# Attention with hashed masks and an FFN on one core: the FFN's chunks start four steps earlier, on a step of their own

## The chip, the cores and the metric

The kernel runs on one core of one Trainium2 chip. Its time is the device time in microseconds (us) of one execution. Three executions of the kernel before took 989.38, 991.98 and 992.04 us; their median is 991.98 us.

## What is computed

For each of 4 batches and 8 heads, attention over 768 positions with 64 numbers per head. A query sees only the keys whose 6 hash bits (signs of a projection) equal its own. The result of the 8 heads, 512 numbers per position, goes through an FFN with 2048 inner units:

```python
q_bits = (np.einsum('bhsd,dk->bhsk', q, proj) > 0).astype(np.int64)
k_bits = (np.einsum('bhsd,dk->bhsk', k, proj) > 0).astype(np.int64)
...
mask = q_bucket[:, :, :, None] == k_bucket[:, :, None, :]
scores = scale * np.matmul(q, k.transpose(0, 1, 3, 2))
scores = np.where(mask, scores, -1000000000.0)
...
attn = attn / (np.sum(attn, axis=-1, keepdims=True) + 1e-09)
return np.matmul(attn, v).astype(np.float32)
...
h = x @ w_in
relu6 = np.clip(h + 3.0, 0.0, 6.0)
g = h * relu6 / 6.0
return (g @ w_out).astype(np.float32)
```

## The kernel before, in words

**Precision.** TensorE multiplies in a reduced float format, so most operands are kept as a high part (a copy, ScalarE mostly) and a low part (the original minus the high part, VectorE or POOL), and products are sums of two or three matrix products. High and low parts are ph/pl for attention weights, xh/xl for the FFN's input, gb or ga (two halves of one tile) for the gated values, kk/qq for a head's keys and queries.

**Attention.** The 32 heads make 192 steps of 128 queries each; step k belongs to head k // 6. `scores` (L376, L378) makes a step's 768 scores s in PSUM; `lowest` (L385, VectorE) copies them to p and finds the extreme; `exponential` (L397, ScalarE) makes the weights. The weights must be transposed. In plain steps TensorE does it: `transp` (L407), six instructions into two banks pt, whose high and low parts are made by L464 (ScalarE) and L468 (VectorE). In mixed steps `flip` does it: VectorE transposes blocks (L418), a DMA writes them to DRAM (fd), and `move` reads them back reordered with four DMAs into one of two homes, spare and px; there ScalarE makes the high parts, VectorE the low part of the first half (L468) and POOL that of the second half (L466). `values` (L489) or `values_whole` (L501) multiply by v for two steps at a time (acc); `output` copies the result to y and DMAs it to the DRAM tensor xs, half of it by an adding DMA that POOL issues (`add`, L510).

**A head's preparation.** The rows raw come by DMA (`get_qk`); a high copy qq (L304), DMAs that move rows between partitions, two low parts kk and qq on POOL (L318), which in mixed steps wait in a list `subs` and are issued one in each odd step; then hash products z (L330 to L332) and hash bits (L341, VectorE).

**FFN.** Its inputs are chunks of 256 positions, three per batch. Batch 0 has its FFN between steps 51 and 52. The nine other chunks come from the generator `ffn`, which the step loop advances piece by piece. `begin` loads a chunk's rows xr from xs and lists small pieces of work in `side`: the reciprocal sums rc (`invert`: L549, L550), then for each of four groups of 128 rows a spread copy of rc on POOL (L559), its transposition rt (L569) and the product xr times rt on VectorE (L572). `split` makes xh (L624) and xl (L625), the low parts in turn on VectorE and POOL. Then come 16 units: `gemm1` (12 matmuls, L635), `gate` (L657 ScalarE, L658 VectorE, L663, L664) and, one unit later, `gemm2` (6 matmuls, L673 to L678). `store` scales the result and DMAs it out.

**What sets the order.** TensorE, VectorE, ScalarE and POOL do their instructions in the order in which the code issues them; SyncE's DMA queue is ordered by a scheduler at build time. Three numbers set the stages: HK = 48, the steps of one batch; GF = 2·HK + FS = 100, from which step on the order within a step changes (`lead` before `split_p`); and GT = GF + FT = 106, the first step whose weights go through `flip` and `move`. From step GT − 1 on, `beside_ffn` runs each step together with one FFN unit; its order within a step is values, `lowest` of step k + 2, the gate's second half (stage A), `exponential` and `flip` of step k + 2, `split_p` of step k − 1, `gemm1` (stage B), hash, `gemm2` and the gate's first half (stage C), scores of step k + 3, moves, a part of `subs`, side work (stage D). The FFN begins when `there(0)` holds: all values of batch 1 done (`vdone >= 96`). In plain steps each call takes one piece of `side` per step; the first `gemm1` of chunk 0 comes in step 106. Chunks 1 to 5 start in steps 122, 138, 154, 170 and 186. What is left after step 194 (55 units) runs alone.

**A detail of buffers.** In plain steps every third half of a step's parts ("extra" in `split_p`) lies in the buffers xh and xl, which the FFN's chunks use too.

Of the kernel before, what the change touches and what calls it, by code (L numbers as in the profile page):

```python
# [18 lines left out]
P = 128  # L19
# [9 lines left out]
LA = 3  # L29
FB = 4  # L30
FS = 4
FT = 6
# [11 lines left out]
def lsh_attention_moe(  # L44
# [10 lines left out]
    nc = tc.nc  # L55
# [384 lines left out]
    def split_p(g: int, c: int, third: bool):  # L440

        nonlocal halves
        u, w = divmod(g, 2)
        if w == 0:
            extra = third and halves % 3 == 2
            halves += 1
            if extra and lent:
                both = [x[:, :S] for x in lent]
            else:
                both = [  # L450
                    sp.tile([P, NCC * TC if extra else S], F32R, name=f"{x}{u}_{c}", tag=f"x{x[1]}" if extra else x, bufs=1 if extra else 2)[:, :S]
                    for x in ("ph", "pl")
                ]
            parts[u, c] = [x.rearrange("p (x w q) -> p x w q", x=QT, w=2) for x in both]
        hi, lo = (x[:, :, w] for x in parts[u, c])
        engine = nc.vector
        if g < GT:
            pt = pts.pop((g, c))[:]
        else:
            pt = moved[g].rearrange("p (i x a) -> p x i a", i=4, x=KT)[:, c * QT : (c + 1) * QT]  # L460
            hi, lo = (x.rearrange("p x (i a) -> p x i a", i=4) for x in (hi, lo))
            if c:
                engine = nc.gpsimd
        nc.scalar.copy(hi, pt)  # L464
        if engine is nc.gpsimd:
            engine.tensor_sub(lo, pt, hi.bitcast(F32))  # L466
        else:
            lows.append(lambda: engine.tensor_sub(lo, pt, hi.bitcast(F32)))  # L468
# [44 lines left out]
    def output(un: int):  # L513
# [16 lines left out]
        else:  # L530
            nc.scalar.copy(y, acc[:])
        if u:
            c = slice(0, 4 * P) if u == 1 else slice(4 * P, S)
            to = xs[b][h * D : (h + 1) * D, c]

            with tc.issue_after(copied.ins):
                dma(out=to, in_=outs[i][r])
            if not last_head:
                adds.append((i, to, outs[i][r2]))
# [25 lines left out]
    def normalise(name: str, x, rb, tag: str | None = None):  # L565
# [6 lines left out]
        muls.append(lambda: nc.vector.tensor_mul(x, x, rt[:]))  # L572
        if not paced:
            multiply()

    muls = []

    def multiply():
# [23 lines left out]
    def scale_x(b: int, t: int, ccs: range, xr, rc=None):  # L602
# [4 lines left out]
        def invert():  # L607
            piece()
            rbs["rc"] = rc if rc is not None else inverse(name, b, slice(t * TC, (t + 1) * TC), ccs)

# [90 lines left out]
    xr0, x0 = {}, {}  # L701
    side = []

# [191 lines left out]
    def ffn():  # L895
# [5 lines left out]
        def there(c: int) -> bool:  # L901

            return vdone >= (chunks[c][0] + 1) * HK

        def begin(c: int):
# [5 lines left out]
            if b < B - 1:  # L911
                side.extend([lambda: None] * (0 if paced else 2) + todo)
                return
# [18 lines left out]
        def split(c: int, cc: int):  # L932
            split_x(xhl[c][cc], xr[c][:, cc], (nc.vector, nc.gpsimd)[cc % 2])

# [70 lines left out]
    def lead(j: int):  # L1005

        i, t = divmod(j, KT)
        n = i + 1
        alone = j < GF + LA
        if t == 0 and n < NJ:  # L1010
# [55 lines left out]
    with tc.manual_schedule(engines={ET.PE, ET.DVE, ET.Activation, ET.Pool}):  # L1066
# [15 lines left out]
        def beside_ffn(k: int):  # L1082

            nonlocal paced, stage
            if k < GT:
# [3 lines left out]
            for _ in range(2):  # L1091
# [8 lines left out]
                if k < GT:  # L1100
                    break
            if k + 2 < NS and k >= GT:
                lowest(k + 2)
# [37 lines left out]

            if subs and k % 2:
                subs.pop(0)()
# [4 lines left out]
        for k in range(NS + LT + 2):  # L1148
# [23 lines left out]
            for _ in range(1 if k != HK else 2):  # L1172
                if vnext < k - k % 2:
                    whole = value_half()
            if k >= GF - 2:
                next(fill, None)
# [7 lines left out]
            for c in range(2):  # L1184
                split_p(k, c, third)
            split_lows()
            if (k < GF or hashed) and k + LA < end:
                if hashed:
# [85 lines left out]
```

## Time and profile before

| | us |
|---|---|
| median of three executions | 991.98 |
| the profiled execution | 993.35 |
| its span, first to last instruction | 991.6 |
| TensorE (PE) busy in the span | 957.5 |
| VectorE (DVE) busy | 716.1 |
| ScalarE (ACT) busy | 626.4 |
| POOL busy | 491.2 |
| mean granted TensorE clock | 0.997 |

Rows of the timeline give an instruction's start, its duration, engine, line of the kernel, operation, tiles written and read, shapes and count; in brackets the idle time of the engine just before and what ended it. Matmuls overlap in the pipe, so a row's duration is longer than the distance to the next start; what a matmul costs is that distance. Rows of the windows give, for a stretch, its length, each engine's busy time and number of instructions, the granted clock, the DMA engines' mean busy share and GB/s.

### The profile page before, as it was taken

Reading aid. Unit: us, or ns where it says so; the run is one execution under the profiler, and the core shown is the slowest. Engines: PE = TensorE matmul, PEld = TensorE weight load, DVE = VectorE, ACT = ScalarE, POOL = GpSimd, SP = SyncE. Lnnn points to the kernel's source line nnn. Section 1 sums busy time; section 2 is a strip of 40 time slices with the busy share of each in tenths; the row PEclk is TensorE's granted clock in tenths of the full one; section 3 lists DMA queues with packets and bytes.
Section 4 is the critical chain, followed back from the end, with each engine's and each line's share of the span. In section 5 each row is a group of like instructions: output and inputs, shape, how many; then the busy total and the mean of one; then the engine's idle time right before and its main releaser. Section 6 shows DMA issues by size and latency. Waiting matters only on the chain.

```text
span 991.6 us, 19371 instructions
## 1 busy us (share of the span) xinstructions
PE 957.5 (97%) x6330; PEld 877.2 (88%) x6330; DVE 716.1 (72%) x1444; ACT 626.4 (63%) x1419; POOL 491.2 (50%) x514
## 2 busy tenths in 40 slices
PE   8999999999999999799999999999999999999997
PEld 7999888999989998699889898888989989899996
DVE  7999988888479998777767877867867863343332
ACT  6888875565488887566656766666666663333332
POOL 6777745666456676365655654645645540000100
PEclk9999999999999999999999999999999999999999
DMA  4566689000035554587888787778788670101000
GB/s 117 137 163 171 141 248 376 9 1 1 27 119 119 120 121 116 139 237 234 235 249 247 221 246 231 226 223 236 240 230 247 202 213 14 43 1 43 1 22 22
DMA packets 109980, 148.51 MB, mean 150 GB/s; under 512 B 13380, under 2 KB 79300, under 8 KB 109880
## 3 DMA queue, kind: packets, MB, share of 16 engines
q1 hardware_dynamic: 105320, 141.64, 47.0%
q0 software_dynamic: 4560, 5.64, 4.7%
q8 instruction: 50, 0.82, 0.4%
q14 instruction: 50, 0.41, 0.1%
HBM read 75.76 MB, written 52.04 MB: 129 GB/s over the span
## 4 chain that ended last, share of the span: by engine, by line
PE 71%; DVE 9%; DMA 7%; POOL 4%; issue 3%; SPq 3%; ACT 2%; DVEq 0%; ACTq 0%; POOLq 0%
PE h L635 23%; PE acc L489 6%; PE po L678 6%; PE po L673 6%; PE po L674 6%; PE pt L407 5%; PE s L376 4%; PE s L378 4%; PE acc L501 4%; DMA px<-fd 3%; SPq L78 3%; DVE p L385 3%; DVE pl L468 3%; POOL pl L466 2%; DMA spare<-fd 2%
## 5 line engine op out<-in xcount | busy, mean ns | idle before, releaser
L397 ACT ACTIVATE p<-p,m 128x768 f32<-128x768 f32 x192 | 180.2, 939 | 94.8 <-DVE p L385 87.8
L385 DVE TENSOR_SCALAR_CACHE_REDUCE p<-s 128x768 f32<-128x768 f32 x192 | 182.9, 953 | 44.3 <-PE s L378 25.7
L658 DVE SCALAR_TENSOR_TENSOR h<-g,h 128x256 f32<-128x256 f32 x192 | 82.0, 427 | 108.2 <-ACT g L657 106.6
L657 ACT ACTIVATE g<-h,three 128x256 f32<-128x256 f32 x192 | 90.8, 473 | 100.0 <-PE h L635 98.2
L635 PE MATMUL h<-xh,w 128*128 128x256 f32 x1024 | 146.4, 282 | 2.7 <-ACT xh L624 2.7
L635 PEld LDWEIGHTS h<-xh,w 128*128 128x128 f32 x1024 | 135.5, 189 | 6.2 <-ACT xh L624 2.9
L418 DVE STREAM_TRANSPOSE p<-p 128x768 f32<-128x768 f32 x86 | 84.1, 978 | 56.9 <-ACT p L397 56.9
L466 POOL TENSOR_TENSOR pl<-spare,ph 128x384 fp32r<-128x384 f32 x43 | 59.1, 1375 | 114.1 <-ACT ph L464 80.1
L468 DVE TENSOR_TENSOR pl<-pt,ph 128x384 fp32r<-128x384 f32 x204 | 104.0, 549 | 3.7 <-ACT ph L464 3.2
L376 PE MATMUL s<-kk,qq 76*128 76x384 f32 x384 | 101.6, 346 | 4.1 <-DVE qq L341 2.3
L378 PE MATMUL s<-kk,qq 128*128 128x384 f32 x384 | 100.5, 343 | 0.0
L464 ACT CAST ph<-pt 128x384 fp32r<-128x384 f32 x204 | 89.5, 472 | 16.6 <-PE pt L407 13.6
L663 ACT CAST gb<-h 128x256 fp32r<-128x256 f32 x139 | 51.6, 372 | 75.6 <-DVE h L658 45.6
L673 PE MATMUL po<-w,gb 128*128 128x512 f32 x246 | 96.9, 394 | 0.2 <-ACT gb L663 0.2
L674 PE MATMUL po<-w,gb 128*128 128x512 f32 x246 | 96.9, 394 | 0.0
L407 PE MATMUL pt<-ident,p 128*128 128x128 f32 x636 | 89.5, 274 | 5.1 <-DVE pl L468 4.1
L216 POOL TENSOR_TENSOR w<-wr,w 128x128 fp32r<-128x128 f32 x128 | 71.8, 591 | 45.3 <-ACT w L210 42.5
L466 POOL TENSOR_TENSOR pl<-px,ph 128x384 fp32r<-128x384 f32 x43 | 58.4, 1357 | 60.0 <-ACT ph L464 40.1
L407 PEld LDWEIGHTS pt<-ident,p 128*128 128x128 f32 x636 | 74.6, 141 | 13.3 <-PE pt L407 3.8
L635 PE MATMUL h<-xl,w 128*128 128x256 f32 x512 | 83.4, 283 | 2.5 <-POOL xl L625 2.2
L376 PEld LDWEIGHTS s<-kk,qq 76*128 76x128 f32 x384 | 65.6, 190 | 16.4 <-DVE qq L341 6.8
L678 PE MATMUL po<-w,gb 128*128 128x512 f32 x246 | 77.4, 395 | 1.6 <-DVE gb L664 1.6
(154 smaller groups left out, 2150.1 us busy)
## 6 DMA issues: line engine op xcount, KB each, us to landing
fd<-p SPq DMA_DIRECT2D x86, 384.0 KB
spare<-fd SPq DMA_DIRECT2D x172, 96.0 KB
px<-fd SPq DMA_DIRECT2D x172, 96.0 KB
kk<-qq SPq DMA_DIRECT2D x62, 192.0 KB
wr<-in_w_in SPq DMA_DIRECT2D x16, 512.0 KB
wr<-in_w_out SPq DMA_DIRECT2D x16, 512.0 KB
raw<-in_qkT SPq DMA_DIRECT2D x20, 384.0 KB
vr<-in_v SPq DMA_DIRECT2D x32, 192.0 KB
```

The source lines that it names most:

```text
L376: nc.tensor.matmul(s[:, c, :HW], lhsT=q1[:KM, us], rhs=half(k1[:KM], c), start=True, stop=False)
L378: nc.tensor.matmul(s[:, c, :HW], lhsT=q2[:, us], rhs=half(k2, c), start=False, stop=True)
L385: nc.vector.tensor_scalar(out=pr_[:], in0=s[:, :, :HW], scalar1=CAP, scalar2=None, op0=ALU.min, op1=ALU.min, accum_out=m[:],)
L397: nc.scalar.activation(pr_[:], pr_[:], AF.Exp, bias=m[:], scale=-1.0, accum_out=sms[b][:, t, h : h + 1])
L407: nc.tensor.transpose(pt[:, x], probs[g][0][:, c, x * P : (x + 1) * P], ident[:])
L466: engine.tensor_sub(lo, pt, hi.bitcast(F32))
L468: lows.append(lambda: engine.tensor_sub(lo, pt, hi.bitcast(F32)))
L635: nc.tensor.matmul(hp, lhsT=wi[:, wp, wc], rhs=x[cc][xp], start=(k == 0 and cc == 0), stop=(k == 2 and cc == NCC - 1),)
L657: nc.scalar.activation(r[:], hp, AF.Relu, bias=three[:], scale=1.0)
L673: nc.tensor.matmul(po[u], lhsT=gh[:, us], rhs=wo[:, 0], start=(fc == 0), stop=False)
L674: nc.tensor.matmul(po[u], lhsT=gh[:, us], rhs=wo[:, 1], start=False, stop=False)
L678: nc.tensor.matmul(po[u], lhsT=gl[:, us], rhs=wo[:, 0], start=False, stop=(fc == NFC - 1))
```

## The change

Several edits go together. FS goes from 4 to 0, so that GF is 96 and GT 102. `there` asks only for the values that a chunk needs (its 256 positions) and that no adding DMA of the batch is outstanding; so that the last head of a batch can be read early, its first 256 positions are written by a DMA of their own. The pieces of a plain-step chunk come without two empty ones ahead (they are behind now), and its `place` and `split` are done at the beginning of step GT, behind that step's values, and not when the generator comes to it. In the steps before GT the multiplications by rt and the reciprocals wait until the step's low parts are issued (`held`, `multiply`). All four xl of a chunk are VectorE's. POOL's part from `subs` is left out in the last step of a chunk and done in the first step of the next. The third half that lies in xh and xl is another one of three.

```diff
-FS = 4
+FS = 0
...
-            extra = third and halves % 3 == 2
+            extra = third and halves % 3 == 1
...
-        if u:
-            c = slice(0, 4 * P) if u == 1 else slice(4 * P, S)
+        if u or last_head:
+            c = slice(2 * u * P, 2 * (u + 1) * P) if last_head and b else slice(0, 4 * P) if u == 1 else slice(4 * P, S)
...
-                dma(out=to, in_=outs[i][r])
+                dma(out=to, in_=y[r] if last_head else outs[i][r])
...
-        if not paced:
+        if not paced and not held:
             multiply()
...
-            rbs["rc"] = rc if rc is not None else inverse(name, b, slice(t * TC, (t + 1) * TC), ccs)
+            def now():
+                rbs["rc"] = rc if rc is not None else inverse(name, b, slice(t * TC, (t + 1) * TC), ccs)
+
+            if held:
+                muls.append(now)
+            else:
+                now()
...
-            return vdone >= (chunks[c][0] + 1) * HK
+            b, t = chunks[c]
+            return vdone >= (b + 1) * HK - KT + 2 * (t + 1) and not any(b * H <= a[0] < (b + 1) * H for a in adds)
...
-                side.extend([lambda: None] * (0 if paced else 2) + todo)
+                side.extend(todo + [lambda: None] * (0 if paced else 2))
+                if not paced:
+                    opening.append(lambda: (place(c), [split(c, cc) for cc in range(NCC)]))
...
-            split_x(xhl[c][cc], xr[c][:, cc], (nc.vector, nc.gpsimd)[cc % 2])
+            split_x(xhl[c][cc], xr[c][:, cc], nc.vector)
...
-        alone = j < GF + LA
+        alone = j <= GF + LA
...
+            if k == GT:
+                opening.pop()()
             if k + 2 < NS and k >= GT:
                 lowest(k + 2)
             go("A")
...
-            if subs and k % 2:
+            place_in_chunk = (k - GT) % NFC
+            if subs and (k % 2 and (k < GT or place_in_chunk != NFC - 1) or k > GT and place_in_chunk == 0):
                 subs.pop(0)()
...
-            if k >= GF - 2:
+            held = k >= GF - 2
+            if held:
                 next(fill, None)
...
             split_lows()
+            multiply()
+            held = False
```

With it chunk 0 begins its loads in step 94 and its units in step 102; chunks 1 to 5 start in steps 118, 134, 150, 166 and 182; four more steps have flipped weights, and 51 units are left for the end. In steps 96 to 99 `lead`, with the hash of head 17 in step 96, now stands ahead of `split_p`.

The order in which instructions stand shows three places. First VectorE where the FFN starts, in the kernel before: p106 and p107 are weights of the first flipped steps, pl52 the last low parts of plain steps, xl1_0 the chunk's low parts, h1_0_0 and gb1_0_0 its first gate.

```order
L468 TENSOR_TENSOR pl52_1_5641<-pt105_1_5649,ph52_1_5640 128x3x128
L418 STREAM_TRANSPOSE p106_5618<-p106_5618 128x768
L385 TENSOR_SCALAR p107_5670,m107_5669<-s107_5632 128x768
L418 STREAM_TRANSPOSE p107_5670<-p107_5670 128x768
L385 TENSOR_SCALAR p108_5708,m108_5707<-s108_5682 128x768
L572 TENSOR_TENSOR xr1_0_5400<-xr1_0_5400,rt1_0_3_5676 128x256
L418 STREAM_TRANSPOSE p108_5708<-p108_5708 128x768
L625 TENSOR_TENSOR xl1_0_5716<-xr1_0_5400,xh1_0_5715 128x256 x2
L658 SCALAR_TENSOR_TENSOR h1_0_0_5725<-g1_0_0_5741,h1_0_0_5725 128x256
L385 TENSOR_SCALAR p109_5755,m109_5754<-s109_5744 128x768
L664 TENSOR_TENSOR gb1_0_0_5757<-h1_0_0_5725,gb1_0_0_5757 128x256
```

The same place in the changed kernel, four steps earlier:

```order
L468 TENSOR_TENSOR pl50_1_5504<-pt101_1_5512,ph50_1_5503 128x3x128
L418 STREAM_TRANSPOSE p102_5486<-p102_5486 128x768
L385 TENSOR_SCALAR p103_5533,m103_5532<-s103_5495 128x768
L418 STREAM_TRANSPOSE p103_5533<-p103_5533 128x768
L632 TENSOR_TENSOR xl1_0_5563<-xr1_0_5271,xh1_0_5562 128x256 x4
L385 TENSOR_SCALAR p104_5573,m104_5572<-s104_5539 128x768
L418 STREAM_TRANSPOSE p104_5573<-p104_5573 128x768
L665 SCALAR_TENSOR_TENSOR h1_0_0_5579<-g1_0_0_5596,h1_0_0_5579 128x256
L385 TENSOR_SCALAR p105_5612,m105_5611<-s105_5601 128x768
L671 TENSOR_TENSOR gb1_0_0_5614<-h1_0_0_5579,gb1_0_0_5614 128x256
```

All four low parts of the chunk have moved ahead of one `lowest` and one `flip`, and the multiplication by rt is gone from this place.

Second POOL where chunk 3 starts (batch 2, positions 0 to 255), before: pl76_1 is the second half's low part of a step, kk_27 and qq_27 the low parts of a head, xl2_0 the chunk's.

```order
L466 TENSOR_TENSOR pl76_1_8616<-spare_5399,ph76_1_8615 128x3x128
L318 TENSOR_TENSOR kk_27_8642<-raw27_8437,qq_27_8643 64x768
L625 TENSOR_TENSOR xl2_0_8657<-xr2_0_8259,xh2_0_8656 128x256 x2
L510 DMA xs3_128<-y24_2_8561 64x256
L466 TENSOR_TENSOR pl76_1_8616<-px_5688,ph76_1_8615 128x3x128
L466 TENSOR_TENSOR pl77_1_8747<-spare_5399,ph77_1_8746 128x3x128
L318 TENSOR_TENSOR qq_27_8643<-raw27_8437,qq_27_8643 64x768
```

And in the changed kernel at the start of the same chunk:

```order
L318 TENSOR_TENSOR kk_26_8377<-raw26_8173,qq_26_8378 64x768
L559 COPY spare_5270<-rc2_0_8131 128x256
L466 TENSOR_TENSOR pl73_1_8351<-px_5544,ph73_1_8350 128x3x128
L466 TENSOR_TENSOR pl74_1_8475<-spare_5270,ph74_1_8474 128x3x128
L466 TENSOR_TENSOR pl74_1_8475<-px_5544,ph74_1_8474 128x3x128
L318 TENSOR_TENSOR qq_26_8378<-raw26_8173,qq_26_8378 64x768
```

POOL has no xl any more, and the head's part that falls into the chunk's last step stands one L466 later.

Third SyncE's DMA queue where a chunk's store, a head's rows and the next chunk's loads meet; before, at the start of chunk 2 (step 138): out is the store, raw25 the rows of a head, xr2_0 the next chunk's loads, px and spare the moves.

```order
L78 DMA raw25_7708<-in_qkT 64x768 x2
L78 DMA fd140_7673<-p140_7666 128x768
L78 DMA xs2_127<-y22_0_7566 64x512
L78 DMA px_5688<-fd139_7612 32x4x192 x2
L78 DMA out_0<-ob1_1_7704 128x512 x2
L78 DMA px_5688<-fd139_7612 32x4x192 x2
L78 DMA xr2_0_8259<-xs2_127 128x256
```

In the changed kernel at the start of chunk 3 (step 150), which has the same place within its head:

```order
L78 DMA out_0<-ob1_2_8560 128x512 x2
L78 DMA px_5544<-fd151_8469 32x4x192 x2
L78 DMA raw27_8564<-in_qkT 64x768
L78 DMA px_5544<-fd151_8469 32x4x192 x2
L78 DMA fd153_8598<-p153_8591 128x768
L78 DMA raw27_8564<-in_qkT 64x768
L78 DMA spare_5270<-fd152_8529 32x4x192
```

The head's rows, which need the buffer that the moved part of `subs` frees, have gone from ahead of the store to behind it, between the moves.

More of the change, by code (lines that the diff above doesn't have):

```diff
@@ L701, in lsh_attention_moe @@
     xr0, x0 = {}, {}
-    side = []
+    side, opening = [], []
     def beside():
@@ L1082, in beside_ffn @@
         def beside_ffn(k: int):
-            nonlocal paced, stage
+            nonlocal paced, stage, held
+            held = False
             if k < GT:
@@ L1186, in lsh_attention_moe @@
             split_lows()
+            multiply()
+            held = False
             if (k < GF or hashed) and k + LA < end:
```

## The prediction

> **What bounds the kernel now.** I read the page first, then the windows, then PE's timeline where a window shows PE idle. The page:
>
> ```profile
> span 991.6 us, 19371 instructions
> PE 957.5 (97%) x6330; PEld 877.2 (88%) x6330; DVE 716.1 (72%) x1444; ACT 626.4 (63%) x1419; POOL 491.2 (50%) x514
> PE   8999999999999999799999999999999999999997
> ```
>
> PE is the bound nearly everywhere: 34.1 us of the span are left beside its 957.5. An edit gains only by removing PE work or PE waits. Of 40 slices one in the middle shows a 7. The windows around it, one of the mixed stage, and one of the end where the FFN runs alone:
>
> ```profile
> 375.00:400.00 25.00, 22.85 (x163) 21.08 (x162) 22.43 (x45) 18.44 (x42) 14.62 (x13) 1.00 0.49 126
> 400.00:425.00 25.00, 18.88 (x118) 16.98 (x118) 18.09 (x37) 13.28 (x32) 10.77 (x11) 0.93 0.55 156
> 500.00:525.00 25.00, 23.59 (x151) 21.14 (x150) 17.25 (x32) 15.07 (x37) 11.34 (x10) 1.00 0.88 248
> 850.00:875.00 25.00, 25.00 (x163) 22.63 (x162) 7.68 (x18) 8.71 (x20) 0.00 (x0) 1.00 0.12 43
> ```
>
> The start of the FFN (375 to 425) holds 2.15 + 6.12 = 8.3 us of idle PE, a quarter of all. A bad window of the mixed stage holds 1.4, the end none. So there are three places where this change can gain: the start, the chunk starts inside the mixed stage, and PE work itself. The third window also warns: its DMA engines are 0.88 busy.
>
> **1. Transpositions that leave PE.** Four steps go over to flipped weights. A plain step's six transpositions, and what starts behind them:
>
> ```profile
> 397.66 0.82 PE L407 MATMUL pt<-ident,p 128*128 128x128 f32 x6
> 398.24 0.61 PE L489 MATMUL acc<-ph,vv 128*128 128x256 f32 x3
> ```
>
> From start to start 0.58 us; four steps give −2.3 us. The FFN units and scores of these steps only change places: PE does them either way. But a mixed step can wait where a unit at the end cannot: the first unit starts at 415.60 in step 106 and the one of step 154 at 639.11 (rows below), 48 steps of 4.66, so four mixed steps are some 19 us; and the windows of the mixed stage lose between 0 and 1.4 per 25. I take the middle, +0.5 (bounds 0 and +1.1).
>
> **2. The start of the FFN.** PE's waits, with the step before the first unit and the first scores behind it:
>
> ```profile
> 394.82 0.52 PE L407 MATMUL pt<-ident,p 128*128 128x128 f32 x3 [1.00 <-DVE pl L468]
> 401.09 0.85 PE L407 MATMUL pt<-ident,p 128*128 128x128 f32 x6 [0.97 <-DVE pl L468]
> 403.20 0.41 PE L569 MATMUL rt<-ident,spare 128*128 128x128 f32 x2 [0.55 <-ACT y L531]
> 410.36 0.44 PE L569 MATMUL rt<-ident,spare 128*128 128x128 f32 x2 [1.48 <-POOL spare L559]
> 412.06 0.87 PE L501 MATMUL acc<-pl,vv 128*128 128x256 f32 x6
> 415.60 2.36 PE L635 MATMUL h<-xh,w 128*128 128x256 f32 x8 [2.67 <-ACT xh L624]
> 418.61 0.84 PE L376 MATMUL s<-kk,qq 76*128 76x384 f32 x2
> ```
>
> The engines that it waited for there, and the granted clock just behind the longest wait:
>
> ```profile
> 393.00 0.98 DVE L549 TENSOR_SCALAR rc<-sms 128x16 f32<-128x16 f32 x1
> 397.94 1.09 DVE L341 TENSOR_SCALAR qq<-z,thr,val 44x768 fp32r<-44x768 f32 x1
> 410.22 0.92 DVE L385 TENSOR_SCALAR_CACHE_REDUCE p<-s 128x768 f32<-128x768 f32 x1
> 413.21 0.92 DVE L385 TENSOR_SCALAR_CACHE_REDUCE p<-s 128x768 f32<-128x768 f32 x1
> 417.50:418.60 1.10, 1.10 (x7) 1.10 (x6) 0.37 (x1) 0.00 (x0) 0.09 (x1) 0.50 1.07 410
> ```
>
> The waits of rt go: all four spread copies now stand on POOL ahead of head 18's preparation, and rt comes at a step's end, behind an output done earlier: −(1.48 + 0.55) = −2.0. The wait of 0.97 had a multiplication by rt ahead of pl; now it stands behind. VectorE is nearly full there (22.43 of 25), so I take half: −0.5. The 1.00 behind rc stays: rc still stands ahead of the next step's pl. New is a wait in step 96, where `lead`, and with it head 17's hash bits of 1.09, now stand ahead of that step's pl; PE's next transpositions need the banks which pl reads. Bounds 0 and +1.1; +0.7, nearer the full row, as the bits also wait for their hash.
>
> The first `gemm1` costs 2.67 of wait and, from 415.60 to 418.61, 3.01 in place of 1.40 (rows below), 4.3 in all. In that chain VectorE goes through one more `lowest`, `exponential` and `flip` round ahead of xh than the changed order does; a round is 413.21 − 410.22 = 3.0. But PE arrives 1.5 earlier, as rt doesn't wait: 2.67 − 3.0 + 1.5 leaves 1.2. Four xh follow one after the other, so the unit itself still runs slower by some 0.9: 2.1 in place of 4.3, −2.2. The round that moved behind is owed by the first gates; PE works on `gemm1` and hash meanwhile, and I take a third of it, +1.0. Sum of the start: −2.0 − 0.5 + 0.7 − 2.2 + 1.0 = −3.0. Bounds: all 8.3 gone, or +1 where new waits outweigh.
>
> The last row shows half the clock granted (0.50) behind that wait; with the wait at 1.2 I count on the full clock, and that is in the 2.1. If the half clock came back, the unit would cost its whole 3.01 − 1.40 = 1.6 over 1.40 and not 0.9, and the start would be −2.3 in place of −3.0. The Trainium skill (TensorE: Matmul & The Clock Gate, Part 1) halves the clock only after an idle window of about 3.4 us. The trace agrees on the half and not on the length: 2.67 of idle were enough. By the page's figure neither 2.67 nor 1.2 should halve it; the row decides, and by it the shorter wait is what matters.
>
> **3. Chunk starts in the mixed stage.** A unit inside a chunk, from its first `gemm1` matmul to its `gemm2`:
>
> ```profile
> 635.61 1.10 PE L635 MATMUL h<-xh,w 128*128 128x256 f32 x8
> 637.01 0.39 PE L673 MATMUL po<-w,gb 128*128 128x512 f32 x1
> ```
>
> 1.40 us. Four of the five chunk starts (122, 138, 154 and 186):
>
> ```profile
> 488.07 1.10 PE L635 MATMUL h<-xh,w 128*128 128x256 f32 x8
> 490.06 0.39 PE L673 MATMUL po<-w,gb 128*128 128x512 f32 x1
> ...
> 562.97 1.10 PE L635 MATMUL h<-xh,w 128*128 128x256 f32 x8
> 566.33 0.39 PE L673 MATMUL po<-w,gb 128*128 128x512 f32 x1
> ...
> 639.11 1.49 PE L635 MATMUL h<-xh,w 128*128 128x256 f32 x8
> 642.56 0.39 PE L673 MATMUL po<-w,gb 128*128 128x512 f32 x1
> ...
> 792.74 1.10 PE L635 MATMUL h<-xh,w 128*128 128x256 f32 x8
> 794.32 0.40 PE L673 MATMUL po<-w,gb 128*128 128x512 f32 x1
> ```
>
> They take 1.99, 3.36, 3.45 and 1.58: 0.6, 2.0, 2.05 and 0.2 too long. The fifth (170) has the place within its head that 122 has, so 0.6: 5.4 together. Why, at 154, with a low part of VectorE's that stood alone (883.59):
>
> ```profile
> 637.21 1.43 POOL L466 TENSOR_TENSOR pl<-spare,ph 128x384 fp32r<-128x384 f32 x1 [2.41 <-PE h L635]
> 638.72 1.82 POOL L318 TENSOR_TENSOR kk<-raw,qq 64x768 fp32r<-64x768 f32 x1
> 640.62 1.67 POOL L625 TENSOR_TENSOR xl<-xr,xh 128x256 fp32r<-128x256 f32 x2
> ...
> 638.81 2.90 DVE L625 TENSOR_TENSOR xl<-xr,xh 128x256 fp32r<-128x256 f32 x2 [0.59 <-ACT xh L624]
> 883.59 0.43 DVE L625 TENSOR_TENSOR xl<-xr,xh 128x256 fp32r<-128x256 f32 x1 [0.47 <-ACT xh L624]
> ```
>
> POOL does the head's part (1.82) first and its two xl after; and VectorE's two take 2.90 beside it, not 2 × 0.43. Now POOL has neither: VectorE needs 4 × 0.43 = 1.7 from 638.8, to 640.5, while PE's eight xh products last to 639.11 + 1.49 = 640.6 at most. I leave 0.3 per start, 1.5, and gain 3.9 of the 5.4, rounded to −3.8 (bounds −5.4 and the rival on POOL below). VectorE's two added xl delay the `lowest` behind them, but that had to wait until 638.81 + 2.90 = 641.7 there, so it is sooner.
>
> The moved part of 1.82 comes a step later. Its hash is another step away, and the next L466 is behind it on POOL. In step 150 the next head's rows need the buffer it frees, and SyncE waits for that with moves behind: 0 to +1.8, I take +0.5.
>
> The five remaining edits cost nothing that I can place: the other third of the buffers is the one that lets xh and xl come free first at step 102; three more small DMAs on SyncE; the end's xl have no partner there.
>
> **Sum.** −2.3 + 0.5 − 3.0 − 3.8 + 0.5 = −8.1. The profiled execution took 993.35 around its span of 991.6; less 8.1 it is 985.2. The median of the three runs lies 1.4 lower, at 991.98, and from there the forecast is **983.9 us**. A difference of 0.3% (3 us) is about what a measurement of this kernel can tell from none.
>
> **The rivals.**
>
> *All goes.* The start's 8.3 and the chunks' 5.4 vanish whole: −2.3 + 0.5 − 8.3 − 5.4 = −15.5, 976.5. For it: some waits stretch PE's rows and aren't in the idle time. Against: rc and bits remain. Chance 0.15.
>
> *POOL's lock.* At 637.21 POOL's pl (1.43) runs just ahead of the chunk's xl. If the chunk's first xl waits for it, as VectorE's did for kk, every start loses up to 1.4, 7.0 in place of 5.4: the term is +1.6 instead of −3.8, and the time 989.3. Against: at 154 it had ended when xh came. Chance 0.08. The Trainium skill (SBUF — State Buffer, Who interferes with whom) has it so: a VectorE instruction with two SBUF inputs and a POOL one that reads SBUF exclude each other for a whole instruction; the row of 2.90 agrees, and by it this change trades one partner for another.
>
> *The moves set the pace.* A mixed step's wait that isn't a chunk start:
>
> ```profile
> 508.47 0.96 DVE L385 TENSOR_SCALAR_CACHE_REDUCE p<-s 128x768 f32<-128x768 f32 x1 [1.75 <-DMA fd<-p]
> 509.83 0.73 PE L678 MATMUL po<-w,gb 128*128 128x512 f32 x2 [1.14 <-DVE gb L664]
> ```
>
> VectorE waits 1.75 for a flipped tile to land, PE 1.14 for VectorE. If DMAs (0.88 busy) hold the stage, PE's chunk starts only wait elsewhere, the 3.8 is lost: 987.7. Against: most windows' DMA share is lower. Chance 0.12.
>
> *Slower: rows between store and loads.* On SyncE a head's rows now stand behind a chunk's store and between moves, at three of the four starts that have heads left to load; rows waiting for POOL hold the moves, and these the casts, VectorE and PE. It decides when it costs over 8.1 in all, 2.0 at each of four starts; a whole part of 1.82, and 1.14 more for VectorE's late fd, make 3.0 each: +12.0, and 995.9. Against: `lowest` has two steps in hand. Chance 0.07.
>
> **How the numbers follow.** The forecast keeps 0.58. Range 977 to 990: it takes in both middle rivals and most of the first, and leaves out the slow one and the first's lower half. Faster by over 3 us (below 989) are nearly all of the forecast (0.56), the first rival (0.15), three quarters of the moves' (4.3 below, 0.09) and a third of the lock's (2.7 below, 0.03): 0.83. The rest of these, 0.02 + 0.03 + 0.05 = 0.10, is within 3 us; slower is the last rival's 0.07.
>
> **What would show it.** Right: 24 transpositions fewer in L407's group; no low part xl on POOL behind 400 us, and 1.4 to 1.9 from `gemm1` to `gemm2` at chunk starts; the first `gemm1` waits below 2 us at a full clock; no slice with a 7. Wrong: long waits of h for xl still (lock); more idle PE behind DVE with releaser fd, px or spare (moves); SyncE held by POOL's L318 (slower).

## The result, and the profile after

The changed kernel takes **981.09 us** (median of 5 executions, 980.28 to 981.59), against 991.98 (989.38 to 992.69, 5 executions) beside it: a ratio of 0.9895, 95% interval 0.9881 to 0.9910. The profiled execution took 981.36. The forecast was 983.9 in a range of 977 to 990. So the change gains 10.9 us where 8.1 were forecast; the sections below show that the chunk starts came out as forecast, the FFN's start only as a sum of parts that missed both ways, and that one term, the other waits of the mixed stage, wasn't in the forecast.

From the page of the kernel after, the span, the engines and PE's slices:

```profile
span 979.6 us, 19386 instructions
PE 953.1 (97%) x6306; PEld 874.4 (89%) x6306; DVE 715.7 (73%) x1462; ACT 626.7 (64%) x1421; POOL 479.2 (49%) x498
PE   8999999999999998899999999999999999999997
```

The slice with a 7 is gone. PE is idle for 26.5 us in place of 34.1, and is busy 4.4 us less.

**Where the 12.0 us of the span went.** The scores of the 192 steps come in order, one L376 row each, so their starts are milestones that both kernels pass. I take those of steps 94 (before the FFN starts), 112 (both kernels are then in mixed steps with one unit each) and 191 (the last). PE's timeline of the kernel before, then of the kernel after (in a second execution of it, from another session, the three rows start at 370.67, 438.95 and 804.44):

```profile
370.72 0.51 PE L376 MATMUL s<-kk,qq 76*128 76x384 f32 x2
...
432.57 0.62 PE L376 MATMUL s<-kk,qq 76*128 76x384 f32 x2
...
804.51 0.52 PE L376 MATMUL s<-kk,qq 76*128 76x384 f32 x2
```

```profile
370.44 0.52 PE L376 MATMUL s<-kk,qq 76*128 76x384 f32 x2
...
439.72 0.62 PE L376 MATMUL s<-kk,qq 76*128 76x384 f32 x2
...
804.27 0.52 PE L376 MATMUL s<-kk,qq 76*128 76x384 f32 x2
```

| us | before | after | after, second | forecast of the difference |
|---|---|---|---|---|
| 94 to 112: FFN's start, four more units in it | 61.85 | 69.28 | 68.28 | |
| 191 to the end: four units fewer | 187.1 | 175.3 | 175.3 | |
| these two together | 248.9 | 244.6 (−4.3) | 243.5 (−5.4) | −2.3 + 0.5 − 3.0 = −4.8 |
| 112 to 191: 79 mixed steps, the same work on PE | 371.94 | 364.55 (−7.4) | 365.49 (−6.5) | −3.8 + 0.5 = −3.3 |

Two executions of one kernel differ by 1 us in a stage, so the first line of differences agrees with the forecast. The mixed stage doesn't: by these traces it gained twice what was forecast. That is more than the medians bear out. The one trace of the kernel before comes from an execution 1.4 above its median, and two edits that change the mixed stage alone bring 4.7 by the medians (below), with 6.9 by the traces. So the gain that was not forecast lies between some 1.5 and 4 us. One execution of an experiment, that with xh and xl behind the round, ran at a granted clock of 0.65 throughout and is left out.

**The start.** PE's waits around the first unit, from the timeline of the kernel after, and a window with the granted clock (the third number from the end):

```profile
401.85 2.36 PE L642 MATMUL h<-xh,w 128*128 128x256 f32 x8 [1.60 <-ACT xh L631]
...
404.86 0.84 PE L376 MATMUL s<-kk,qq 76*128 76x384 f32 x2
...
408.72 0.40 PE L330 MATMUL z<-qq,pjl 128*108 128x384 f32 x1 [1.05 <-DVE p L385]
...
412.66 0.62 PE L376 MATMUL s<-kk,qq 76*128 76x384 f32 x2 [1.26 <-DVE qq L341]
```

```profile
402.60:405.50 2.90, 2.90 (x13) 2.78 (x13) 2.19 (x6) 0.27 (x2) 0.00 (x0) 0.51 0.71 266
```

The wait for xh fell from 2.67 to 1.60, but the half clock came all the same (0.51), and the unit takes 404.86 − 401.85 = 3.01, just as before. Behind it two new waits stand, 1.05 and 1.26.

**Chunk starts.** Three of the five in the kernel after, first `gemm1` matmul and first `gemm2` matmul:

```profile
476.55 1.50 PE L642 MATMUL h<-xh,w 128*128 128x256 f32 x8
...
478.35 0.40 PE L680 MATMUL po<-w,gb 128*128 128x512 f32 x1
...
626.10 1.10 PE L642 MATMUL h<-xh,w 128*128 128x256 f32 x8
...
627.50 0.39 PE L680 MATMUL po<-w,gb 128*128 128x512 f32 x1
...
700.64 1.49 PE L642 MATMUL h<-xh,w 128*128 128x256 f32 x8
...
702.43 0.39 PE L680 MATMUL po<-w,gb 128*128 128x512 f32 x1
```

They take 1.80, 1.40 and 1.79, the other two 1.54 each: 1.1 in all over 1.40, where 1.5 was allowed and 5.4 stood before.

**The other waits of the mixed stage.** PE's waits from 425 to 810, first of the kernel before, then after (total, times, longest):

```profile
PE s L376 <- DVE qq L341: 2.3, 3, 1.5
PE h L635 <- POOL xl L625: 2.2, 6, 1.2
PE acc L501 <- POOL pl L466: 1.6, 7, 0.3
PE po L678 <- DVE gb L664: 1.6, 2, 1.1
```

```profile
PE acc L501 <- POOL pl L466: 1.8, 8, 0.3
PE s L376 <- DVE qq L341: 1.7, 4, 0.5
```

PE no longer waits for xl, as forecast, nor in this execution for gb, which wasn't forecast; and its longest wait for the hash bits (qq) is 0.5 in place of 1.5.

### The profile page after: what moved, and what is told of

Its sections match the earlier page's. It is cut to its first block, busy times and chain, and to the rows that moved or that the text cites. A ratio compares the mean times of both kernels' runs of the same rounds, so it can differ in the third digit from the quotient of the medians.

```text
span 979.6 us, 19386 instructions
## 1 busy us (share of the span) xinstructions
PE 953.1 (97%) x6306; PEld 874.4 (89%) x6306; DVE 715.7 (73%) x1462; ACT 626.7 (64%) x1421; POOL 479.2 (49%) x498
## 4 chain that ended last, share of the span: by engine, by line
PE 77%; DVE 9%; issue 4%; POOL 3%; DMA 3%; ACT 2%; SPq 1%; DVEq 0%; ACTq 0%; POOLq 0%
PE h L642 25%; PE po L685 6%; PE po L680 6%; PE po L681 6%; PE acc L489 6%; PE acc L501 5%; PE s L376 5%; PE pt L407 5%; PE s L378 5%; DVE p L385 3%; DVE pl L468 2%; POOL pl L466 2%; DVE qq L341 1%; DMA px<-fd 1%; SPq L78 1%
## 5 line engine op out<-in xcount | busy, mean ns | idle before, releaser
L418 DVE STREAM_TRANSPOSE p<-p 128x768 f32<-128x768 f32 x90 | 88.0, 978 | 60.3 <-ACT p L397 60.3
L466 POOL TENSOR_TENSOR pl<-spare,ph 128x384 fp32r<-128x384 f32 x45 | 62.1, 1381 | 119.0 <-ACT ph L464 82.8
L376 PE MATMUL s<-kk,qq 76*128 76x384 f32 x384 | 101.4, 345 | 4.8 <-DVE qq L341 3.0
L468 DVE TENSOR_TENSOR pl<-pt,ph 128x384 fp32r<-128x384 f32 x196 | 100.0, 550 | 3.6 <-ACT ph L464 3.0
L681 PE MATMUL po<-w,gb 128*128 128x512 f32 x250 | 98.4, 394 | 0.0
L680 PE MATMUL po<-w,gb 128*128 128x512 f32 x250 | 98.4, 394 | 0.0
L466 POOL TENSOR_TENSOR pl<-px,ph 128x384 fp32r<-128x384 f32 x45 | 61.3, 1362 | 75.2 <-ACT ph L464 66.0
L464 ACT CAST ph<-pt 128x384 fp32r<-128x384 f32 x196 | 85.9, 472 | 15.1 <-PE pt L407 13.1
L407 PE MATMUL pt<-ident,p 128*128 128x128 f32 x612 | 86.0, 274 | 3.6 <-DVE pl L468 2.7
L407 PEld LDWEIGHTS pt<-ident,p 128*128 128x128 f32 x612 | 71.7, 141 | 11.2 <-PE pt L407 2.5
L376 PEld LDWEIGHTS s<-kk,qq 76*128 76x128 f32 x384 | 65.7, 190 | 17.9 <-DVE qq L341 8.0
L685 PE MATMUL po<-w,gb 128*128 128x512 f32 x250 | 78.7, 395 | 0.0
```

What stands on the lines that cost most here:

```text
L376: nc.tensor.matmul(s[:, c, :HW], lhsT=q1[:KM, us], rhs=half(k1[:KM], c), start=True, stop=False)
L407: nc.tensor.transpose(pt[:, x], probs[g][0][:, c, x * P : (x + 1) * P], ident[:])
L680: nc.tensor.matmul(po[u], lhsT=gh[:, us], rhs=wo[:, 0], start=(fc == 0), stop=False)
L681: nc.tensor.matmul(po[u], lhsT=gh[:, us], rhs=wo[:, 1], start=False, stop=False)
L685: nc.tensor.matmul(po[u], lhsT=gl[:, us], rhs=wo[:, 0], start=False, stop=(fc == NFC - 1))
```

## The experiments

All times are medians of 4 to 12 executions (`before` in these sessions: 991.34, 991.37 and 991.15). Where waits are summed over the mixed stage, they are what the distance between matmul starts exceeds the distance that the shape takes unhindered, worked out from all of PE's rows. They are kept apart as those of the first units of the five chunks, of the second units, and all others. A unit counts here with the values and scores of its step, so the first units lose more than the 1.1 above. Each row but the times comes from one execution; those of before, of the head part's edit and of the head part in every odd step took 1.4 to 1.5 us more than the median, that of the xl edit 1.8 less.

| kernel | us | 112 to 191 | first units | second units | other waits |
|---|---|---|---|---|---|
| before | 991.98 | 371.94 | 5.5 | 1.9 | 17.7 |
| after | 981.09 | 364.55 | 1.8 | 3.7 | 12.9 |
| after, second | 981.69 | 365.49 | 1.8 | 3.6 | 13.8 |
| after, FS = 4 | 982.31 | 364.79 | 1.3 | 3.8 | 12.8 |
| after, two xl on POOL | 981.56 | 364.88 | 2.6 | 2.4 | 13.6 |
| after, head part in every odd step | 983.68 | 368.09 | 6.0 | 4.4 | 11.4 |
| before with both edits of POOL | 986.67 | 365.02 | 1.3 | 3.9 | 13.0 |
| before with the head part's edit | 987.39 | 365.29 | 2.2 | 2.4 | 13.9 |
| before with the xl edit | 989.67 | 367.09 | 4.2 | 4.2 | 11.8 |
| after, bits ahead of the gate | 977.24 | 362.01 | 1.6 | 3.5 | 10.6 |

Two theories stood against each other at first for the unforeseen gain. The **phase theory**: with FS = 0 the chunks start at other places within a head, and the stage runs better for that. The **POOL theory**: the edits that take work off POOL at a chunk's start relieve more than the start. The kernel after was run again beside the kernels of the last session:

> The kernel after, unchanged, as the measure for the three beside it on the same chip: 981.1 us, and PE's waits in the same places as before, the first gemm1 at half clock behind some 1.6 us of wait.

It took 981.69 (980.55 to 982.91), with the first `gemm1` behind 1.60 of wait and then the half clock again.

### Put the shift back: FS = 4

```diff
-FS = 0
+FS = 4
```

> The changed kernel (981.1 us) with FS = 4 again: the FFN starts in step 106 as before, every other edit stays. Phase theory: of the 10.9 us gained, some 5 came because the four steps moved the heads' row loads away from the chunks' stores and loads, so that flipped tiles land in time; undone, these waits come back (+5) beside four steps of transpositions (+2.3): 988.4. POOL theory: those 5 came because POOL, without low parts and head parts at chunk starts, keeps the moves in time; the shift alone is worth its transpositions, so 983.4.

982.31 us, ratio to before 0.9907 (0.9892 to 0.9923). The phase theory falls: with the old phase the mixed stage takes 364.79, the same as after. The shift itself is worth 0.6 to 1.2 by the medians, whose intervals overlap, and by the trace's start and end together (244.6 or 243.5 against 59.49 + 186.45 = 245.9) 1.3 to 2.4; −2.3 + 0.5 was the forecast of it.

### Both edits of POOL alone, on the kernel before

```diff
-            split_x(xhl[c][cc], xr[c][:, cc], (nc.vector, nc.gpsimd)[cc % 2])
+            split_x(xhl[c][cc], xr[c][:, cc], nc.vector)
...
-            if subs and k % 2:
+            place_in_chunk = (k - GT) % NFC
+            if subs and (k % 2 and (k < GT or place_in_chunk != NFC - 1) or k > GT and place_in_chunk == 0):
```

> The kernel before (992.0 us) with two edits alone: all xl of chunks 1 to 8 on VectorE, and POOL's head part moved out of a chunk's last step; FFN start and its four steps as before. Phase theory: only the chunk starts gain, -3.8: 988.2. POOL theory: the waits for flipped tiles go as well, another -5: 983.2.

986.67 us, 0.9950 (0.9936 to 0.9963): 4.7 off, less than the POOL theory's 983.2, but the whole gain of the mixed stage is there (365.02). What is left to the kernel with FS = 4, 4.4 us, is the start's new order and a little at the end. From step 94 to 112 the two differ by 61.79 − 59.49 = 2.3; kernels with the old order differ there by up to 2.0 (61.62 to 63.62), so the trace alone doesn't show that part.

### Two of the four xl back on POOL

```diff
-            split_x(xhl[c][cc], xr[c][:, cc], nc.vector)
+            split_x(xhl[c][cc], xr[c][:, cc], (nc.vector, nc.gpsimd)[cc % 2])
```

> The changed kernel with a chunk's low parts again in turn on VectorE and POOL, the rest as changed (POOL's head part still leaves the chunk's last step). Phase theory: only the chunk starts lose; without the head part ahead of POOL's two xl each start is like the mild ones of before (0.6 over 1.40, now some 0.35), so +1.3: 982.4. POOL theory: POOL's later moves cost some 2.5 of the 5 us as well: 985.

981.56 us, 0.9897 (0.9882 to 0.9913): no difference that can be measured. The first units lose 0.8 more in all, but the second units 1.3 less. With four xl on VectorE PE is through with the first unit sooner, but the low part pl that the next step needs comes no sooner: at the start of step 118 POOL begins it 3.97 us behind the first `gemm1` (476.55 to 480.52) and here 3.91 (475.69 to 479.60).

### The head part back in every odd step

```diff
-            if subs and (k % 2 and (k < GT or place_in_chunk != NFC - 1) or k > GT and place_in_chunk == 0):
+            if subs and k % 2:
```

> The changed kernel with POOL's head part in every odd step as before, all four xl on VectorE. Three of five chunk starts (from steps 117, 149, 165) then have a head part of 1.82 us beside VectorE's four xl. If the two exclude each other as in the kernel before (2.90 us for two xl), VectorE's xl come up to 1.8 us later, PE's first unit waits some 1.3 more at each: +4, 985. If the exclusion was POOL's own queue and not VectorE's wait: 981.1. POOL theory adds up to 2.5: 987.

983.68 us, 0.9918 (0.9903 to 0.9933): 2.0 to 2.6 given back. The chunk start of step 118, from the timelines of this kernel and of the kernel after:

```profile
476.40 1.83 POOL L318 TENSOR_TENSOR kk<-raw,qq 64x768 fp32r<-64x768 f32 x1
476.49 3.04 DVE L632 TENSOR_TENSOR xl<-xr,xh 128x256 fp32r<-128x256 f32 x4 [0.60 <-ACT xh L631]
476.79 1.49 PE L642 MATMUL h<-xh,w 128*128 128x256 f32 x8
...
478.57 1.39 PE L642 MATMUL h<-xl,w 128*128 128x256 f32 x4 [0.29 <-DVE xl L632]
```

```profile
476.24 1.43 DVE L632 TENSOR_TENSOR xl<-xr,xh 128x256 fp32r<-128x256 f32 x4 [0.60 <-ACT xh L631]
```

Four xl take 3.04 beside POOL's head part and 1.43 without it, a difference about as long as the head part: one of the four takes 2.03, the others 0.41, so it waits the head part out, and PE stands behind. The same shows at three of the five starts. The Trainium skill (SBUF — State Buffer, Who interferes with whom) has the shared port pair of VectorE and POOL as an exclusive lock; these rows agree with it.

### Each edit of POOL alone, on the kernel before

The head part's rule alone, and then the xl alone (each the half of the diff above).

> The kernel before, with the head part of a chunk's last step put off by one step and nothing else. Theory, POOL has too much at a chunk's start and either relief is enough: first units of the chunks lose some 2.6 in all in place of 5.5, the other waits of the mixed stage fall from 17.7 to some 13.5, and the time is 986.5 us. Rival, each of the two edits frees its own share: half of the 4.7 that both gave, 989.0 us, with the other waits at some 15.5. Rival, the low parts of xl are what counts: 991 us.

987.39 us, 0.9960 (0.9948 to 0.9972): 4.0 of the 4.7. The other waits fall to 13.9, as the theory that POOL has too much had it.

> The kernel before, with all four xl of a chunk on VectorE and nothing else. Theory, either relief of POOL is enough: the other waits of the mixed stage fall from 17.7 to some 12, but chunk starts with a head part in the step ahead still lose some 1.8 each, 6.0 in all, and the second units some 2 more: 988.0 us. Rival, each of the two edits frees its own share: the other waits at some 15.5 and 989 to 990 us. Rival, the head part is what counts: the other waits stay at 17.7 and the second units make it slower: 993 us.

989.67 us, 0.9983 (0.9975 to 0.9992): 1.7 of the 4.7. The other waits fall here too, to 11.8, where "either is enough" had some 12, but the starts keep 4.2 and the second units take 4.2. So for the other waits either edit is enough. For the time neither "either is enough" nor "each its own half" is right: the head part's edit brings nearly all, and the xl edit next to nothing beside it (0.7).

One chunk start shows how a wait at POOL becomes waits elsewhere. Step 154 begins alike in both kernels: POOL's pl starts at 637.21 in the kernel before (its row stands in the prediction) and at 637.12 with the head part moved. What follows on VectorE, on SyncE's queue (SPq) and at the next scores that need hash bits, first before:

```profile
641.63 0.94 DVE L385 TENSOR_SCALAR_CACHE_REDUCE p<-s 128x768 f32<-128x768 f32 x1
...
650.82 0.38 SPq L78 DMA_DIRECT2D fd<-p  x1
652.92 0.32 SPq L78 DMA_DIRECT2D xr<-xs  x1
653.36 2.32 SPq L78 DMA_DIRECT2D spare<-fd  x4
...
659.49 1.09 DVE L341 TENSOR_SCALAR qq<-z,thr,val 44x768 fp32r<-44x768 f32 x1
...
660.63 0.62 PE L376 MATMUL s<-kk,qq 76*128 76x384 f32 x2 [1.54 <-DVE qq L341]
```

The same instructions with the head part moved:

```profile
640.00 0.94 DVE L385 TENSOR_SCALAR_CACHE_REDUCE p<-s 128x768 f32<-128x768 f32 x1
...
648.12 0.38 SPq L78 DMA_DIRECT2D fd<-p  x1
648.60 2.05 SPq L78 DMA_DIRECT2D spare<-fd  x4
...
656.26 1.08 DVE L341 TENSOR_SCALAR qq<-z,thr,val 44x768 fp32r<-44x768 f32 x1
...
657.40 0.62 PE L376 MATMUL s<-kk,qq 76*128 76x384 f32 x2
```

`lowest` is 1.6 earlier, the write of the flipped tile 2.7, the moves 4.8, the hash bits 3.2 and the scores 3.2. PE lost 1.54 of that three steps behind the chunk start, where the forecast counted nothing, and another 1.5 ahead of the scores of step 164.

The rows show a second thing. In the kernel before a load of the next chunk's rows (xr) stands in SyncE's queue ahead of the moves, and is issued at 652.92, 1.7 after the row ahead of it has ended. With the edit it isn't there. No edit touches SyncE, but its queue is ordered when the kernel is built, and the edit on POOL put the loads behind the next moves at this chunk start and at that of step 138:

```
 DMA out_0<-ob1_2 128x512
 DMA fd157<-p157 128x768
-DMA xr2_1<-xs2 128x256
 DMA spare<-fd156 32x4x192 x4
 DMA raw28<-in_qkT 64x768 x2
-DMA xr2_1<-xs2 128x256
 DMA fd158<-p158 128x768
...
 DMA px<-fd157 32x4x192 x4
+DMA xr2_1<-xs2 128x256 x2
```

SyncE's waits for a chunk's stores to land, 425 to 810, in the kernel before and with the xl moved (1.5 with the head part moved, 1.0 in the kernel after):

```profile
SPq L78 <- DMA out<-ob: 5.4, 5, 1.9
```

```profile
SPq L78 <- DMA out<-ob: 1.6, 2, 0.9
```

Is it the late VectorE or the queue that PE waits for behind the start? The kernel with the xl moved tells them apart at step 154: the head part still holds VectorE's xl (3.04), but the queue's order at this place is that of the kernel with the head part moved. The same instructions in it, behind a first `gemm1` at 637.21:

```profile
639.87 0.94 DVE L385 TENSOR_SCALAR_CACHE_REDUCE p<-s 128x768 f32<-128x768 f32 x1
...
648.17 0.38 SPq L78 DMA_DIRECT2D fd<-p  x1
648.68 1.97 SPq L78 DMA_DIRECT2D spare<-fd  x4
...
656.13 1.09 DVE L341 TENSOR_SCALAR qq<-z,thr,val 44x768 fp32r<-44x768 f32 x1
...
657.28 0.62 PE L376 MATMUL s<-kk,qq 76*128 76x384 f32 x2
```

Counted from the first `gemm1`, `lowest` begins at 2.66, as late as in the kernel before (2.52; 0.99 with the head part moved), and POOL's next pl at 5.63 (5.44 before). The moves begin at 11.47 in place of 14.25, the scores at 20.07 in place of 21.52, and PE waits neither here nor ahead of the scores of step 164. So at this start the two later waits, 3.1 us together, are missing though VectorE and POOL are as late as before; they go with the order of the queue.

The table agrees: with the head part back in every odd step the first and second units lose 10.4, more than the 7.4 of the kernel before, and the other waits are still 11.4. This was read at one start, from one execution of each kernel, and no kernel here held the queue's order fixed while it changed POOL; how much of the other waits elsewhere is the queue's stays open.

### The start: scores ahead of the first gemm1

```diff
+            if k == GT:
+                lead(k + LA)
             go("B")
...
-            if k + LA < NS:
+            if k + LA < NS and k != GT:
                 lead(k + LA)
```

In step GT the first unit's `gemm1` is issued in `go("B")`.

> The kernel after, with one thing moved: in the FFN's first step the scores that stood behind the first gemm1 stand ahead of it. In the kernel after PE waits 1.60 us for xh there and then runs the gemm1 at a granted clock of 0.50. Theory that the length of the idle time brings the half clock: the scores (0.7 us) fill the wait to some 0.9, the clock stays at 1.00, and the unit from gemm1 to the next scores takes some 1.5 in place of 3.0: 979.0 us, if nothing behind it is late. Rival, VectorE sets the pace of the start: the clock recovers, but the hash of head 18 and the scores behind it wait longer for p and for the hash bits by as much, and the time is 980.5 to 981.1. Rival, the half clock comes from the load that begins and not from the wait: granted 0.50 behind the shorter wait too, and 980.8.

982.36 us, 0.9909 (0.9896 to 0.9921): no gain. The timeline and two windows of the start:

```profile
402.88 1.78 PE L642 MATMUL h<-xh,w 128*128 128x256 f32 x8 [0.37 <-ACT xh L631]
...
409.43 0.39 PE L330 MATMUL z<-qq,pjl 128*108 128x384 f32 x1 [2.73 <-DVE p L385]
```

```profile
402.88:405.10 2.22, 2.22 (x12) 1.75 (x13) 2.02 (x6) 0.87 (x3) 0.00 (x0) 1.00 0.93 324
...
410.60:413.00 2.40, 2.40 (x8) 1.92 (x6) 2.37 (x4) 0.98 (x3) 1.66 (x2) 0.50 0.90 241
```

Behind the short wait the clock stays full, so here the half clock went with the wait and not with the `gemm1` that begins. But the time is not won: the hash waits 2.73 for `lowest` where it waited 1.05, and the half clock comes there. VectorE sets the pace of the start, as the first rival had it, which named 980.5 to 981.1 for the time.

### The start: xh and xl behind the round

```diff
-                if not paced:
-                    opening.append(lambda: (place(c), [split(c, cc) for cc in range(NCC)]))
...
-            if k == GT:
-                opening.pop()()
```

PE's order stays the same.

> The kernel after, with the first chunk's xh and xl behind the step's lowest, exponential and flip on ScalarE and VectorE in place of ahead of them; PE's order is the same. Theory, this order is worth what it takes off PE's wait: PE waits some 2.9 in place of 1.60 for xh, then half clock as before; the waits behind it (1.05 for p at the hash, 1.26 for the bits at the scores) stay: 982.4 us. Rival, the round is only owed later: the wait grows by 1.3, those behind it shrink by as much, and the time stays at 981.1.

983.60 us, 0.9921 (0.9908 to 0.9933). The kernel ran a second time for its trace:

> The kernel after, with the first chunk's xh and xl behind the step's lowest, exponential and flip, as once before (983.6 us then); this time for its trace and beside the kernel after. Theory, the round stands in PE's way twice: PE waits some 2.9 for xh in place of 1.60, the half clock stays, and the waits behind it do not shrink by as much, 1.5 to 2.5 us slower than the kernel after. Rival, the round is only owed later: within 0.5 us of it.

983.94 us against 981.69 beside it. The timeline of VectorE, ScalarE and PE:

```profile
404.92 0.96 DVE L385 TENSOR_SCALAR_CACHE_REDUCE p<-s 128x768 f32<-128x768 f32 x1 [1.47 <-DMA fd<-p]
...
406.90 0.69 ACT L631 CAST xh<-xr 128x256 fp32r<-128x256 f32 x2
...
407.34 0.58 PE L642 MATMUL h<-xh,w 128*128 128x256 f32 x1 [6.16 <-ACT xh L631]
```

PE waits 6.16, far more than the 2.9 expected: a wait of VectorE for a flipped tile (1.47) and the whole round stand ahead of xh now. The wait of the hash behind it vanishes and pays back a part: the wait for xh is 4.6 longer, the time 2.3. So the order that `opening` sets is worth 2.3 us by the medians of one session.

### A better version: hash bits ahead of the gate

In the mixed stage the scores and the hash share one pair of banks, so scores wait until VectorE has read the hash out of it.

```diff
             if hashed:
                 hash_qk((k + LA) // KT + 1)
-            go("C")
             if hashed:
                 bits((k + LA) // KT + 1)
+            go("C")
```

> The kernel after, with the hash bits of a head ahead of the gate on VectorE in the 14 steps of the FFN that make them. PE's order is the same. Theory, what is left of the waits in these steps is the one pair of banks, which the scores get back only when VectorE has read the hash out of it: of the 3.8 us that scores wait behind a gemm2 in the kernel after, some 3 go, and it is 978.5 us. Rival, VectorE's order only passes the delay on: the gate comes 1.1 us later, gemm2 of the next step or the next lowest waits instead, and it stays at 980.5 to 981.5.

**977.24 us**, ratio to before 0.9864 (0.9849 to 0.9879), against 0.9903 (0.9889 to 0.9917) of the kernel after in the same session: 4.4 us faster than it, and faster than the kernel before and the kernel after. The waits of the scores from 425 to 810, the kernel after in that session and this one:

```profile
PE s L376 <- DVE qq L341: 1.2, 3, 0.5
```

```profile
PE s L376 <- DVE qq L341: 0.2, 1, 0.2
```

The mixed stage from scores 112 to 191 takes 362.01, 3.5 less than in that execution of the kernel after and 2.5 less than in the first. One us of it is in these rows. The distances from a `gemm2` to the scores behind it, against the median for that shape, show more: they exceed it by 2.9 and 2.3 in the two executions of the kernel after and by 0.7 here, so 1.6 to 2.2 us are the scores' waits, as the theory had it, if somewhat less than its 3.

> The kernel of the bits ahead of the gate, and two of a chunk's four xl on POOL again. Theory, with the head part moved off, which engine makes the xl does not matter: within 0.7 us of the kernel with the bits alone. Rival, POOL's xl bring back SyncE's backlog at chunk starts: 3 us more than it.

(The same with the xl edit of POOL taken back.) 980.18 us, 0.9882 (0.9867 to 0.9898). The median is 2.9 above, as the rival had it, and the mixed stage 2.1 longer, but the intervals overlap: it only leans against POOL's xl. SyncE's waits for the stores are 2.1 in place of 1.0; they are 2.1 as well in the kernel after with two xl on POOL, which lost nothing, so the backlog that the rival gives as the cause is not shown.

## Why the prediction was right, and where it wasn't

**Transpositions, −2.3, with +0.5 for four more mixed steps.** Right: L407 counts 612, 24 fewer, and the shift taken back costs 1.3 to 2.4 by the trace.

**The start, −3.0.** Right as a sum, and partly by luck, not in its parts. The total of start and end is −4.3 and −5.4 in two executions, −4.8 by the forecast. The waits of rt (2.03) became one of 1.05 in one execution and 0.30 in the other; the wait in step 96, priced at +0.7, came with 0.98. The first `gemm1` was to gain 2.2; the wait was 1.60 and not 1.2, and "the full clock" that I counted on didn't come, so it gained 1.1. That is the branch that the prediction named and priced. The moved round was to cost a third of itself, +1.0; the two waits behind it are 2.3 and 2.0. What covered these misses are the waits of the transpositions for pl: they fell from 3.5 to 1.9 in both executions, the new 0.98 among them, −1.6 where −0.5 + 0.7 was forecast. The 1.00 behind rc, which was to stay, is gone: rc now starts right behind a pl (378.69), and beside the 0.98 no wait for pl is above 0.33. All of PE's listed waits from 372 to 428 sum to 8.3 before and 6.9 and 5.9 after.

**Chunk starts, −3.8.** Right in size (5.4 became 1.1) and in cause, but too broad: I credited both edits, and the head part alone brings most of it (2.1 are left with it alone, 3.2 with the xl alone). With it back, VectorE's four xl take 3.04; with two xl back on POOL, no time is lost. And the change has a price that I put at nothing or less, since "VectorE's two added xl delay the `lowest` behind them, but that had to wait": the pl behind them comes no sooner than PE needs it, and second units lose 1.8 more.

**The moved part of `subs`, +0.5.** It cost nothing that shows; SyncE's waits for it in the mixed stage are 0.2 after and 0.9 before.

**The term that was mis-sized** is the zero for the other waits of the mixed stage. The prediction quoted VectorE's wait of 1.75 for a flipped tile and PE's of 1.14, and used them for a rival by which the gain would be lost. They were not a fixed floor: in the traces 17.7 of such waits became 12.9 to 13.8, and either edit of POOL alone does it (13.9 and 11.8). They do not simply follow a late chunk start, as 11.4 beside first and second units that lose 10.4 shows; where it could be read, at step 154, they follow the moves that SyncE's queue holds behind the loads. With that sized, the forecast would have been 1.5 to 4 lower. The total came within 2.8 of the result because the other terms together agreed with it.

**The rivals.** POOL's lock came with pl at one start of five, that of step 150: pl ran from 624.21 for 1.43, the xl began at 625.11 and the first took 0.81, and the unit still took 1.40. (At those of steps 134 and 182 the first xl took 1.10 beside another subtraction of POOL's, L357, and the units 1.54.) With the head part the lock is real (3.04 against 1.43). "The moves set the pace" was wrong in sign: PE did wait for moves, at step 154 for ones that stood behind a load in SyncE's queue, but these waits shrank with the change instead of eating its gain. "Slower" did not come about: SyncE's order changed, but for the better.

## What to carry to other kernels

When too much stands at one point, look a few steps behind for its other costs: here the waits that followed were about as large as those at the place itself, and they bore other names (a DMA, a hash, a gate). Which engine or queue they follow is seen in a kernel where one of the two is late and the other isn't; here that was the xl edit alone. Price an instruction on VectorE by what POOL does at that moment, and move what can be moved by a step rather than to another engine. And where a queue is ordered at build time, an edit on one engine may reorder another's; read both orders before crediting the edit.

## What the runs showed of the hardware

At the start, the half clock came behind the waits of 1.60 and 2.73 us (0.51 and 0.50 in the windows shown), and not behind 0.37 (1.00). Behind the wait of 1.26 that ended at 412.66 it was 1.00 too, in the kernel after:

```profile
412.60:413.60 1.00, 0.94 (x6) 0.94 (x7) 0.00 (x1) 0.00 (x0) 1.00 (x2) 1.00 0.90 331
```

The Trainium skill (TensorE: Matmul & The Clock Gate, Part 1) has an idle window of about 3.4 us; in this kernel half of that is enough. What counts may be the work of a longer stretch and not one gap; no run here separates that. Two things speak for it: in the kernel before the wait of 1.54 that ended at 660.63 was followed by 1.00 (660.60 to 664.00), though it is nearly as long as 1.60, and the half clock does not begin with the `gemm1` at 401.85 in the kernel after but lasts from 402.67 to 406.08, with 1.00 behind it.
